# A list scheduler told that four transposes land late, a new shuffle seed, and an unevenly split last output tile

## The chip, the cores and the metric

One core of one Trainium2 chip runs the whole program. The metric is the device time of one execution in microseconds; the kernel before has a median of 276.47 us over three runs (277.43, 276.40, 276.47). The profiled execution, from whose trace all views here are taken, has a span of 275.7 us from first to last instruction, and a mean granted TensorE clock of 0.999.

## The reference

The input x has 2048 tokens of width 640. It is layer-normalised once, and two branches read the normalised xn; their sum is added to x.

```python
x  = A_x
xn = _layernorm(x, axis=-1)
return x + _A_ref(xn, A_wqkv, A_w_phi, A_wo) + _B_ref(xn, B_w1, B_w3, B_w2)

# A: linear attention, 32 heads of 20: q, k, v from xn @ wqkv
phi_q = concat(softmax(q @ w_phi), softmax(-(q @ w_phi)))     # the same for k
kv, z = phi_k^T v, sum over tokens of phi_k
o     = phi_q kv / (phi_q z + 1e-6);  return o @ wo

# B: gated MLP, 640 -> 1536 -> 640
h = silu(xn @ w1) * (xn @ w3);        return h @ w2
```

## The kernel before

**Tiling.** Tokens are cut into 16 tiles of 128, and into 4 blocks of 512. Work for the matrix engine (TensorE, PE in the profile) comes in units, each of which owns one, two or four of the eight PSUM banks. Those that matter here are:

- V and K of a token tile: five chunks of the model width times two halves of 320 columns, 10 matmuls each. They read xnT (the normalised tokens, transposed) and the weights wv and Wkp (wk with w_phi folded in). ScalarE and VectorE drain them to v2 and ekt.
- MLP units "M block.chunk", made by `mlp` (line 1046): 5 matmuls of 512 columns with w1 and 5 with w3, all on one block's xnT. ScalarE makes a tanh, VectorE two products, and the result goes to hT. Units M0.0 to M0.11 belong to block 0, which holds token tiles 0 to 3 only. Unit M0.f reads columns 128f to 128f+127 of w1 and w3.
- kv_sum, kv_back, q_proj and q_tok: the attention itself.
- output tiles O0 to O15, made by `out_tile` (line 1064): 12 chunks of hT times w2 and 5 chunks of oT times wo, times two column groups, 34 matmuls. VectorE adds the residual, and SyncE (SP) stores the tile.

**Start.** Tiles 0 to 3 are transposed on PE. Tiles 4 to 15 are normalised in place in x_tok by `ln_apply`, and then turned by a transposing DMA (`turn`, lines 692, 1165 and 1166) from x_tok into xnT. All these DMAs are on SP's queue, beside the loads of later x tiles, of w1 and w3 (`load_w13`, in pieces of 384 columns, that is three M units each) and the transposing loads of wq and wk (wqkT).

**What sets the order.** The order of each engine's instructions is not written out by hand. `_Program.schedule` (line 171) is a list scheduler with a cost model: it takes every operation's modelled duration, keeps a modelled end for each, and at each step commits the piece of work that can start first. Among those that can start within a small slack, the one with the higher level goes. Levels are due times: `when(us)` is 1000 - us, so V of tile t has due time 20 + 5(t - 4), K the same plus 2, and M0.f 24 + 5f (lines 1178, 1179 and 1193). The slack is drawn at random from a seeded generator up to a modelled time of 175 us; that is what SEED (line 496) decides. For a DMA, the model adds a fixed 1.3 us plus the operation's own `extra` to the modelled end of its transfer:

```python
692    def turn(o, i, level=0.0, dram=False, after=()):
...
695        d.extra = 1.0 if dram else 0.2
```

`extra` is a number inside the model only. Nothing on the chip waits because of it; it moves the point at which the model lets a unit that reads the turned tile be committed. `emit` then writes one fixed list of instructions for each engine, with semaphore waits for the true dependences, and each engine plays its list in order. The 12 DMA-turned tiles have `extra` 0.2.

**The end.** The last output tile, O15, is computed as two separate units of bank work: the first 320 columns with all 17 chunks, then the other 320, each followed by its own addition on VectorE and its own store, so that the first store runs under the second half's matmuls.

Of the kernel before, what the change touches and what calls it, by code (L numbers as in the profile page):

```python
# [5 lines left out]
ALU = mybir.AluOpType  # L6
# [4 lines left out]
D = 640  # L11
# [3 lines left out]
T = S // 128  # L15
# [477 lines left out]
CENTRED = {0: "ACT", 1: "ACT", 2: "ACT", 3: "DVE"}  # L493
POOLED = ()
TURNED = ()
SEED = 65
TRIPLES = ((0, 3, 0, 60), (3, 3, 60, 60), (6, 3, 120, 60), (9, 3, 180, 60), (12, 3, 240, 60), (13, 3, 300, 20))


def bass_parallel_sum__linear_kernel_hedgehog__glu_gated_swiglu__prompt_kernel(  # L500
# [13 lines left out]
    P = _Program(nc)  # L514
# [12 lines left out]
    def new(name, shape, dtype, offset=None):  # L527
        size = mybir.dt.size(dtype)
        for n in shape[1:]:
            size *= n  # L530
        return P.sbuf(name, shape, dtype, region(size) if offset is None else offset)
# [23 lines left out]
    xres = new("xres", [128, 4, D], bf)  # L555
# [42 lines left out]
    def bank(k, cols=512, off=0, p0=0, p1=128):  # L598
        return PS[p0:p1, k * 512 + off:k * 512 + off + cols]

    def bank2(k, cols):
        return PS[:, k * 512:(k + 2) * 512].rearrange("p (b c) -> p b c", c=512)[:, :, 0:cols]

    def free(ap):
        n = 1
        for s in ap.shape[1:]:
            n *= s
        return n
# [6 lines left out]
    def mm(j, o, l, r, start, stop, shared=False, busy=None):  # L615
        u, n = P.unit, free(r)

        def emit():
            return nc.tensor.matmul(o(u.k), l, r, start=start, stop=stop, skip_group_check=shared)  # L619
        return P.mm(emit, [l, r], j, max(n / 2400 + 0.0025, 0.035) if busy is None else busy, n)  # L620

    def way(eng, name, args, kw, busy, lat):
        u = P.unit
        e = {"ACT": nc.scalar, "DVE": nc.vector, "POOL": nc.gpsimd}[eng]

        def emit():
            return getattr(e, name)(*[at(a, u) for a in args], **{k: at(v, u) for k, v in kw.items()})  # L627
        emit.__name__ = name
        return eng, (emit, busy, lat)
# [5 lines left out]
    def sb(*aps):  # L635
        return [a for a in aps if hasattr(a, "ap")]

    def add(ways, w, r, banks=None, level=0.0, after=(), part=False):
        o = P.op(dict(ways), sb(*w), sb(*r), banks, level, after)
        o.part = part  # L640
        return o
# [11 lines left out]
    def w_tt(eng, o, a, b, f, n, fast=1):  # L653
        if eng == "DVE":
            return way(eng, "tensor_tensor", (o, a, b, f), {}, 0.07 + n / 960 / fast, 0.15 + n / 960 / fast)
        return way(eng, "tensor_tensor", (o, a, b, f), {}, 0.14 + n * 1.7 / 1000, 0.18 + n * 1.7 / 1000)
# [25 lines left out]
    def pieces(o, elem):  # L682
        n = 1
        for s in o.shape:
            n *= s
        return n * 2 / elem / 16, max(18.5, 12 + 0.04 * elem) / 1e3

    def load(o, i, level=0.0, eng="SP", after=()):
        return P.dma(eng, lambda: queue[eng].dma_start(o, i), sb(o), sb(i), *pieces(o, 2 * o.shape[-1]), 0.45, level,  # L689
                     after)  # L690

    def turn(o, i, level=0.0, dram=False, after=()):
        d = P.dma("SP", lambda: nc.sync.dma_start_transpose(o, i), sb(o), sb(i), *pieces(o, 256),
                  1.31, level, after)
        d.extra = 1.0 if dram else 0.2
        return d
# [4 lines left out]
    out_t = out.rearrange("b (t p) d -> p (b t) d", p=128)  # L701
# [18 lines left out]
    def load_wT(which, e, level, after=()):  # L720
        return turn(wqkT[:, which * DC + e:which * DC + e + 1, :],
                    A_wqkv[:, which * D + 128 * e:which * D + 128 * e + 128], level, True, after)
# [42 lines left out]
    def ln_stats(t0, n, level):  # L765
        for t in range(t0, t0 + n):
            for q in range(2):
                i, o = x_tok[:, t, 320 * q:320 * q + 320], bst[:, t, 6 * q:6 * q + 6]
                add([w_op("DVE", "bn_stats", (o, i), 0.48, 0.5)], [o], [i], None, level)
            o, i = mv[:, t, 0:2], bst[:, t, 0:12]  # L770
            add([w_op("DVE", "bn_aggr", (o, i), 0.13, 0.21)], [o], [i], None, level)
        m, v, r, z = mv[:, t0:t0 + n, 0], mv[:, t0:t0 + n, 1], mv[:, t0:t0 + n, 4], mv[:, t0:t0 + n, 6]
        add([w_op("POOL", "tensor_scalar_add", (r, v, EPS), 0.21, 0.25)], [r], [v], None, level)
        add([w_op("POOL", "tensor_tensor", (r, r, mhalf[:, 0:n], ALU.pow), 0.55 + 0.1 * (n - 1),
                  0.6 + 0.1 * (n - 1))], [r], [r, mhalf[:, 0:n]], None, level)
        if t0 >= 4:
            add([w_op("POOL", "tensor_scalar_mul", (z, m, -1.0), 0.21, 0.25)], [z], [m], None, level)
            add([w_op("POOL", "tensor_tensor", (z, z, r, ALU.mult), 0.21, 0.25)], [z], [z, r], None, level)

    def ln_apply(t, level):  # L780
        o, m, s, z = x_tok[:, t, :], mv[:, t, 0:1], mv[:, t, 4:5], mv[:, t, 6:7]
        ways = [w_op("DVE", "tensor_scalar", (o, o, m, s, ALU.subtract, ALU.mult), 0.35, 0.44)]
        if t in POOLED:
            ways = [w_op("POOL", "tensor_scalar", (o, o, m, s, ALU.subtract, ALU.mult), 2.5, 2.55)]
        if t >= 4:
            ways.append(w_act(o, o, ACT.Identity, D, s, z))
        add(ways, [o], [o, m, s, z] if t >= 4 else [o, m, s], None, level)
# [274 lines left out]
    finish = []  # L1062

    def out_tile(t, level):
        b, ti = divmod(t, 4)
        u = P.begin(2, level, stream="O")
        u.name = f"O{t}"
        chunks = [(hT[b][:, i, ti * 128:(ti + 1) * 128], w2_s, i) for i in range(FC)]
        chunks += [(oT[:, i, t * 128:(t + 1) * 128], wo_s, i) for i in range(DC)]
        r = xres[:, t % 4, :].rearrange("p (b c) -> p b c", c=320)  # L1070
        load(xres[:, t % 4, :], x_t[:, t, :], 2e5 - 2 * t)
        if t < 4:
            P.all[-1].early = 60.0
        last = t == T - 1
        for qs in ([(0,), (1,)] if last else [(0, 1)]):
            for n, (l, w, i) in enumerate(chunks):
                for q in qs:
                    mm(q, lambda k, q=q: bank(k + q, 320), l, w[:, i, 320 * q:320 * q + 320], n == 0,
                       n == len(chunks) - 1)
            if last:  # L1080
                q = qs[0]
                add([w_tt("DVE", r[:, q, :], lambda k, q=q: bank(k + q, 320), r[:, q, :], ALU.add, 320)],
                    [r[:, q, :]], [r[:, q, :]], [q], 2e6)
                finish.append(load(out_t[:, t, 320 * q:320 * q + 320], r[:, q, :], 3e5))
            else:
                if qs[0] == 0:
                    add([w_tt("DVE", r, lambda k: bank2(k, 320), r, ALU.add, D)], [xres[:, t % 4, :]],
                        [xres[:, t % 4, :]], [0, 1], 1e6)
                    finish.append(load(out_t[:, t, :], xres[:, t % 4, :], 3e5 - 2 * t))

    def filler(t, until):
        u = P.begin(1, 0.0)
# [36 lines left out]
    for e in range(DC):  # L1129
        o = load_wT(1, e, lv - 9 - e, first)  # L1130
    load_x(4, 8, lv - 19, "SP", [o])
    n = len(P.all)
# [14 lines left out]
    n = len(P.all)  # L1147
# [13 lines left out]
    for t in range(4, T, 2):  # L1161
        ln_stats(t, 2, 1e5 - t)
        ln_apply(t, 2e5 - t)
        ln_apply(t + 1, 2e5 - t)
        turn(xnT[:, :, t * 128:(t + 1) * 128], x_tok[:, t, :], lv)
        turn(xnT[:, :, t * 128 + 128:(t + 2) * 128], x_tok[:, t + 1, :], lv)

    def when(us):
        return 1000.0 - us
# [11 lines left out]
    n = len(P.all)  # L1181
# [8 lines left out]
    for b in range(3):  # L1190
        for fc in range(FC):
            n = 12 * b + fc
# [6 lines left out]
    for b in range(NB):  # L1199
        for j in range(4):  # L1200
            t = 4 * b + j
# [4 lines left out]
    for t in range(T):  # L1206
        out_tile(t, when(200 + 5 * t))

    P.schedule({"PE": 1.25, "ACT": 1.12, "DVE": 0.93, "POOL": 0.8, "SP": 0.81}, filler, 12.0, SEED, 175.0)

# [60 lines left out]
```

The softmax here doesn't subtract the row's maximum and nothing guards it: scores larger than these inputs give would overflow.

## Time and profile before

| what | value |
|---|---|
| median time, range of three | 276.47 us, 276.40 to 277.43 us |
| span of the profiled execution | 275.7 us |
| VectorE, ScalarE, GpSimd busy | 183.7, 102.8, 60.4 us |
| DMA traffic | 21.98 MB, mean 80 GB/s |
| V of tile 4 starts on PE | 39.06 us |
| last matmul's result ready | about 273.05 us |

The span is split into 40 slices of 6.9 us in the page's busy rows, where a digit is tenths of the slice. "Idle before, releaser" is the time that an engine stood still ahead of an instruction, and what ended that wait by the trace's semaphore events; where several semaphores were waited for, the one named is the one that came last near that moment, and it can be a bystander. "To landing" of a DMA counts from its issue to the moment when its semaphore is complete.

### The profile page before, as it was taken

How to read it: one execution, taken by the hardware profiler on the slowest of the kernel's cores; microseconds unless marked ns; L12 is line 12 of the kernel's file. 1: busy time of each engine (PE TensorE's matmuls, PEld its weight loads, DVE VectorE, ACT ScalarE, POOL GpSimd, SP SyncE). 2: the span in 40 equal slices, each digit the busy share in tenths (PEclk: the TensorE clock that was granted, in tenths of full speed). 3: DMA queues.
4: the chain of work that ended last, by engine and by line, in shares of the span. 5: the costliest groups of instructions: out<-in, count | busy, mean ns of one | idle time of the engine just before them, and what ended most of it. 6: DMA issues, size and time to landing. Idle time of an engine off the chain costs nothing.

```text
span 275.7 us, 5062 instructions
## 1 busy us (share of the span) xinstructions
PE 267.7 (97%) x2085; PEld 159.5 (58%) x2104; DVE 183.7 (67%) x322; ACT 102.8 (37%) x188; POOL 60.4 (22%) x101
## 2 busy tenths in 40 slices
PE   8999979999999999999999999999999999999996
PEld 4747437765664446644444445777677774444774
DVE  5848886999999544478759986277677215666212
ACT  6637618874445441237393364010110002322000
POOL 4500632699989800000000000000000000000000
PEclk9999999999999999999999999999999999999999
DMA  7568998672000000702131111234443322000001
GB/s 233 153 95 275 343 165 174 106 205 74 0 0 2 0 0 2 259 30 26 24 50 22 26 26 26 71 95 75 108 111 84 85 71 74 0 0 0 26 24 48
DMA packets 41287, 21.98 MB, mean 80 GB/s; under 512 B 27056, under 2 KB 41264, under 8 KB 41264
## 3 DMA queue, kind: packets, MB, share of 16 engines
q1 hardware_dynamic: 40688, 21.01, 31.4%
q10 hardware_dynamic: 576, 0.66, 0.7%
q8 instruction: 16, 0.26, 0.4%
q14 instruction: 7, 0.06, 0.1%
HBM read 12.81 MB, written 2.62 MB: 56 GB/s over the span
## 4 chain that ended last, share of the span: by engine, by line
PE 90%; DVE 4%; DMA 2%; issue 1%; ACT 1%; ACTq 0%; DVEq 0%
PE PS L619 89%; DMA x_tok<-in_A_x_dram 2%; DVE hT L627 1%; DVE t L627 1%; DVE prod L627 1%; DVE bst L627 0%; PE PS L857 0%; DVE den_s L627 0%; ACTq L689 0%; DVE Wqp L627 0%; ACT th L627 0%; ACT EqT L627 0%; ACT L627 0%; DVE xres L627 0%; ACT e_s L627 0%
## 5 line engine op out<-in xcount | busy, mean ns | idle before, releaser
L619 PE MATMUL PS<-xnT,w_s 128*128 128x512 bf16 x464 | 104.9, 379 | 1.2 <-issue 0.5
L619 PEld LDWEIGHTS PS<-xnT,w_s 128*128 128x128 bf16 x480 | 46.4, 98 | 54.1 <-DVE hT L627 0.3
L619 PE MATMUL PS<-w_s,hT 128*128 128x320 bf16 x384 | 55.0, 299 | 0.0
L627 ACT ACTIVATE th<-PS 128x512 f32<-128x512 f32 x48 | 28.7, 599 | 63.9 <-PE PS L619 63.7
L627 DVE SCALAR_TENSOR_TENSOR t<-th,PS 128x512 bf16<-128x512 f32 x48 | 32.9, 684 | 26.2 <-ACT th L627 26.0
L619 PEld LDWEIGHTS PS<-w_s,hT 128*128 128x128 bf16 x384 | 37.0, 98 | 14.9
L627 POOL TENSOR_TENSOR ekt<-ekt,rS 128x640 bf16<-128x640 bf16 x32 | 39.6, 1272 | 1.9 <-DVE rS L627 1.9
L627 DVE TENSOR_TENSOR xres<-PS,xres 128x640 bf16<-128x640 f32 (+1 forms) x17 | 13.4, 786 | 39.0 <-PE PS L619 39.0
L627 DVE SCALAR_TENSOR_TENSOR hT<-t,PS 128x512 bf16<-128x512 bf16 x48 | 32.6, 679 | 1.3 <-DVE t L627 0.2
L627 ACT ACTIVATE EqT<-PS 128x512 bf16<-128x512 f32 x40 | 21.9, 595 | 12.0 <-PE PS L619 12.0
L627 ACT ACTIVATE e_s<-PS 128x64 f32<-128x64 f32 x32 | 9.1, 284 | 44.3 <-PE PS L619 43.9
L619 PE MATMUL PS<-wo_s,oT 128*128 128x320 bf16 x160 | 24.5, 299 | 0.0
L627 DVE TENSOR_TENSOR prod<-PS,g_s 128x1280 bf16<-128x1280 f32 x16 | 23.9, 1491 | 0.5
L619 PE MATMUL PS<-Wkp,xnT 128*128 128x320 bf16 x160 | 23.9, 299 | 0.0
L627 ACT ACTIVATE ekt<-PS 128x640 bf16<-128x640 f32 x32 | 20.8, 702 | 7.7 <-PE PS L619 7.5
L619 PE MATMUL PS<-xnT,Wqp 128*128 128x512 bf16 x97 | 22.9, 379 | 0.3 <-issue 0.2
L627 DVE TENSOR_REDUCE S<-ekt 128x64 f32<-128x1280 bf16 x16 | 22.8, 1450 | 0.0
L619 PE MATMUL PS<-wv,xnT 128*128 128x320 bf16 x120 | 18.3, 299 | 1.9 <-DVE mv L627 1.9
L619 PEld LDWEIGHTS PS<-wo_s,oT 128*128 128x128 bf16 x160 | 15.7, 98 | 6.1
L619 PEld LDWEIGHTS PS<-Wkp,xnT 128*128 128x128 bf16 x160 | 15.5, 98 | 6.1 <-ACT Wkp L627 0.2
L627 DVE BATCH_NORM_STATS2 bst<-x_tok 128x6 f32<-128x320 bf16 x32 | 14.2, 472 | 3.9 <-DMA x_tok<-in_A_x_dram 3.8
L619 PEld LDWEIGHTS PS<-wv,xnT 128*128 128x128 bf16 x120 | 11.7, 98 | 7.5 <-DVE mv L627 2.4
(69 smaller groups left out, 167.2 us busy)
## 6 DMA issues: line engine op xcount, KB each, us to landing
w_s<-in_B_w_dram SPq DMA_DIRECT2D x8, 480.0 KB, 7.5
xres<-in_A_x_dram SPq DMA_DIRECT2D x16, 160.0 KB, 2.2
out_dram<-xres SPq DMA_DIRECT2D x15, 160.0 KB, 1.8
x_tok<-in_A_x_dram SPq DMA_DIRECT2D x3, 640.0 KB, 7.6
w_s<-in_B_w_dram SPq DMA_DIRECT2D x1, 1920.0 KB, 8.9
wo_s<-in_A_wo_dram SPq DMA_DIRECT2D x1, 800.0 KB, 5.1
x_tok<-in_A_x_dram SPq DMA_DIRECT2D x2, 160.0 KB, 3.6
x_tok<-in_A_x_dram ACTq DMA_DIRECT2D x2, 160.0 KB, 4.4
```

Of the source, the lines that this page charges most:

```text
L619: return nc.tensor.matmul(o(u.k), l, r, start=start, stop=stop, skip_group_check=shared)
L627: return getattr(e, name)(*[at(a, u) for a in args], **{k: at(v, u) for k, v in kw.items()})
```

## The change

Three edits. First, the transposes of token tiles 4 to 7 (the loop runs over tile pairs 4-5, 6-7 and so on) get `extra` = 8.0 in place of 0.2, so that the scheduler believes that they land 7.8 us later than before. V and K of tile 4 then look unready for longer, and the scheduler fills the time with MLP units of block 0, whose tiles are there: units M0.3 to M0.9 go ahead of V and K of tile 4, where M0.3 to M0.6 did before. It is meant to bring the model's landing nearer to the chip's. Second, the seed of the shuffled slack is another one, which may reorder any close decision before 175 us of modelled time. Third, the last output tile is cut 384 and 256 columns, not 320 and 320, so that what follows the last matmul is a smaller addition and a smaller store. The rest of the diff in `out_tile` is the same code in another shape: tiles 0 to 14 are as before.

```diff
-SEED = 65
+SEED = 1008
...
-        last = t == T - 1
-        for qs in ([(0,), (1,)] if last else [(0, 1)]):
+        if t < T - 1:
             for n, (l, w, i) in enumerate(chunks):
-                for q in qs:
+                for q in range(2):
                     mm(q, lambda k, q=q: bank(k + q, 320), l, w[:, i, 320 * q:320 * q + 320], n == 0,
                        n == len(chunks) - 1)
-            if last:
-                q = qs[0]
-                add([w_tt("DVE", r[:, q, :], lambda k, q=q: bank(k + q, 320), r[:, q, :], ALU.add, 320)],
-                    [r[:, q, :]], [r[:, q, :]], [q], 2e6)
-                finish.append(load(out_t[:, t, 320 * q:320 * q + 320], r[:, q, :], 3e5))
...
+            return
+        for q, c0, c1 in ((0, 0, 384), (1, 384, D)):
+            for n, (l, w, i) in enumerate(chunks):
+                mm(q, lambda k, q=q, c=c1 - c0: bank(k + q, c), l, w[:, i, c0:c1], n == 0, n == len(chunks) - 1)
+            o = xres[:, t % 4, c0:c1]
+            add([w_tt("DVE", o, lambda k, q=q, c=c1 - c0: bank(k + q, c), o, ALU.add, c1 - c0)], [o], [o], [q], 2e6)
+            finish.append(load(out_t[:, t, c0:c1], o, 3e5))
...
         turn(xnT[:, :, t * 128:(t + 1) * 128], x_tok[:, t, :], lv)
         turn(xnT[:, :, t * 128 + 128:(t + 2) * 128], x_tok[:, t + 1, :], lv)
+        if t < 8:
+            for d in P.all[-2:]:
+                d.extra = 8.0
```

More of the change, by code (lines that the diff above doesn't have):

```diff
@@ L1073, in out_tile @@
             P.all[-1].early = 60.0
-        last = t == T - 1
-        for qs in ([(0,), (1,)] if last else [(0, 1)]):
+        if t < T - 1:
             for n, (l, w, i) in enumerate(chunks):
-                for q in qs:
+                for q in range(2):
                     mm(q, lambda k, q=q: bank(k + q, 320), l, w[:, i, 320 * q:320 * q + 320], n == 0,
                        n == len(chunks) - 1)
-            if last:
-                q = qs[0]
-                add([w_tt("DVE", r[:, q, :], lambda k, q=q: bank(k + q, 320), r[:, q, :], ALU.add, 320)],
-                    [r[:, q, :]], [r[:, q, :]], [q], 2e6)
-                finish.append(load(out_t[:, t, 320 * q:320 * q + 320], r[:, q, :], 3e5))
[L1085 to L1089, printed above, removed]
+            add([w_tt("DVE", r, lambda k: bank2(k, 320), r, ALU.add, D)], [xres[:, t % 4, :]],
+                [xres[:, t % 4, :]], [0, 1], 1e6)
+            finish.append(load(out_t[:, t, :], xres[:, t % 4, :], 3e5 - 2 * t))
+            return
[5 more added lines that the diff above has]
+            finish.append(load(out_t[:, t, c0:c1], o, 3e5))
     def filler(t, until):
```

## Prediction

> **What bounds the kernel now.** I read the page's shares first, then PE's waits, then PE's timeline around the longest wait, then the landings of the DMAs that this wait hangs on, and last the end of the timeline.
>
> ```profile
> PE 267.7 (97%) x2085; PEld 159.5 (58%) x2104; DVE 183.7 (67%) x322; ACT 102.8 (37%) x188; POOL 60.4 (22%) x101
> PEclk9999999999999999999999999999999999999999
> PE 90%; DVE 4%; DMA 2%; issue 1%; ACT 1%; ACTq 0%; DVEq 0%
> ```
>
> PE is busy for 97% of the span at full clock and is 90% of the chain that ended last: only PE's idle time and its number of columns can be saved. The change leaves the columns alone, so everything lies in 275.7 - 267.7 = 8.0 us of idle time. By stretches it is:
>
> ```profile
> 14.70:28.50 13.80, 13.73 (x99) 1.00 0.79 202
> 28.50:37.10 8.60, 8.56 (x39) 1.00 1.14 273
> 37.10:39.06 1.96, 0.02 (x1) 1.00 1.35 144
> 39.06:107.00 67.94, 67.42 (x420) 1.00 0.30 65
> 107.00:175.00 68.00, 67.10 (x670) 1.00 0.22 52
> 175.00:273.03 98.03, 97.86 (x757) 1.00 0.22 59
> 273.03:275.70 2.67, 0.00 (x0) 0.89 0.11 31
> ```
>
> (Columns: stretch, its length, PE busy with instructions, clock, DMA share, GB/s.) One hole of 1.94 us stands out, the tail is 2.67, and from 39 to 175 us some 1.4 us lie in crumbs. The hole on PE's timeline:
>
> ```profile
> 28.54 8.58 PE L619 MATMUL PS<-xnT,w_s 128*128 128x512 bf16 x39
> 39.06 1.52 PE L619 MATMUL PS<-wv,xnT 128*128 128x320 bf16 x10 [1.94 <-DVE mv L627]
> 40.42 1.52 PE L619 MATMUL PS<-Wkp,xnT 128*128 128x320 bf16 x10
> ```
>
> These are M0.3 to M0.6 (40 matmuls, 39 recorded), then V and K of tile 4, V of tile 5 and so on. V of tile 4 reads xnT of tile 4. The releaser named, a VectorE statistic, only fell at that moment: V doesn't read it. The transpose of that tile, asked for alone, reads
>
> ```profile
> L693 SPq DMA_TRANSPOSE xnT<-x_tok x1: 3127/3127/3127, 28.9 to 28.9; - x1
> DMA to landing us min/median/max: 10.0/10.0/10.0
> ```
>
> so it was issued at 28.95 and landed near 38.95, 0.1 us before V starts. A transpose issued at 44.4 lands in 2.7 us: this one was late because the queue ahead of it was full. The last x load (25.46, 10.4 us to landing) and a w1 load (27.12, 10.1 us) were still moving, and the DMA share was above 1.
>
> **What the Trainium skill says.** "DMA: Bandwidth & Descriptors", section on queues, rings and completion order: on each DMA engine descriptors are consumed in ring order. The 10.0 against 2.7 us agrees. "TensorE: Matmul & The Clock Gate", section on what happens when you issue a matmul: matmuls stay in program order, only weight loads are pulled ahead; so one unready V stops the M units listed behind it. The hole agrees. The same page, section on the back-to-back gap: N/2.4 + 2.5 ns; for 512 columns 216 ns, and the trace has 8.58 us for 40, 215 ns; for 320 columns 136 ns, and the trace has 10 per 1.36 us.
>
> **The change, part by part.**
>
> 1. *M0.7 to M0.9 go ahead of V4.* This adds no work: three units of 10 x 0.215 = 2.15 us, 6.45 us in all, come forward from after 61 us. M0.3 to M0.9 run from 28.54 to 28.54 + 7 x 2.15 = 43.6. The transposes of tiles 4 to 7 were issued at 28.95, 32.07, 35.7 and 37.1 and took 10.0, 7.8, 4.9 and 4.1 us: landed at 38.95, 39.9, 40.6 and 41.2. All precede 43.6, so V4 waits for nothing: -1.94 us.
>
> 2. *What the units need.* w1 and w3 columns 768 to 1151 (M0.6 to M0.8) landed at 22.5 + 8.5 = 31.0 and 23.9 + 10.2 = 34.1; M0.7 starts at 37.1, free. M0.9 needs columns 1152 on: w1 landed at 27.12 + 10.1 = 37.2. The w3 piece was issued only after the four transposes, at 38.55, and landed 4.1 us later, at 42.65. M0.9 starts at 28.54 + 6 x 2.15 = 41.4, its w3 half at 42.5: a new wait of some 0.15 us if SP keeps its order. Queued behind it are the second half of M0.9 and then V4; all of PE would wait. Bounds 0 (w3 goes earlier) and, if all four wqkT transposes issued after it (39.18 to 44.33) went first, 5.15 us more. I take +0.15, since both have the same inputs and levels as before.
>
> 3. *VectorE and ScalarE.* Three units bring 3 x (0.684 + 0.679) = 4.1 us of VectorE forward. From 37.1 to 43.6 VectorE was busy 3.9 of 6.5 us, so about 1.5 us of statistics and norms are pushed back. Who waits: the later transposes and with them V8. It ran at 49.9 with its transpose landed at 44.4 + 2.7 = 47.1; now it runs some 4.5 us later, at 54.4. Even a delay of all 4.1 us is hidden. In return 60 to 70 us, where VectorE was 9.9 of 10 us busy and PE waited 0.26 us for Wqp, gets lighter: 0 to -0.26, I take -0.1.
>
> 4. *K norms.* GpSimd's norms start up to 4.5 us later; they ended at 95.4 and kv_sum starts at 107.2: hidden.
>
> 5. *Last tile.* 17 x (162.5 + 109.2) ns = 17 x 2 x 135.8 = 4.62 us: no change on PE. The first part ends 17 x 64/2400 = 0.45 us later, its addition and store lie under the 1.86 us of the second: nothing. Behind the last matmul: latency 299 ns at 320 columns, and by the slope to 379 at 512 it is 272 at 256, -0.03. The addition: 0.49 us at 320 and 0.82 at 640, so 0.43 at 256, -0.07. The store moves 64 in place of 80 KB; at the 340 GB/s that the core moved from 30 to 33 us that is -0.05, or nothing if its 1.6 us are all latency; I take -0.02. Its rows become 512 bytes, the least that "DMA: Bandwidth & Descriptors", specifications, gives for full rate; no run here shows smaller ones. Sum -0.12, bounds -0.1 to -0.15.
>
> 6. *The seed.* It redraws near ties up to 175 us. What it can win is bounded by the crumbs: 0.5 + 0.9 us from 39 to 175, and 0.1 from 14.7 to 37. What it can lose the profile does not bound: any unready unit in an in-order queue is a new hole, and the 1.94 us is the one size that I have for one. I take 0, with about 0.8 us either way.
>
> Sum: -1.94 + 0.15 - 0.1 - 0.12 = -2.0. From 276.47, **274.5 us**, 0.7% faster.
>
> **The rivals.**
>
> *The hole is partly given back.* Order is redrawn everywhere, and crumbs of 0.16 us (there are four such waits "for issue") or a wait of half the old size return, about 1.2 us. For it: the model that misjudged tile 4 still judges all else. Against: from 39 to 273 us PE always had a ready unit in its list, 1.6 us idle in 234, and M units of other blocks remain as fill. It gives 275.7, no difference that can be told.
>
> *The wait moves to the w3 piece of M0.9.* If SP puts it behind two of the wqkT transposes, it lands 2 x 1.28 = 2.6 us later, and PE waits 2.7 us where it waited 1.94. For it: SP was held 9.6 us by four transposes, so it runs late and the piece has only -0.15 us of slack. Against: the piece went before them. With the gain at the tail and a little lost to the seed this gives 277.3, slower; with all four ahead, 276.5 + 5.15 - 1.8 = 279.8.
>
> *The start shortens too.* Up to 14.7 us PE is filled with dummy matmuls between the first tiles, and another draw can bring M0.0 forward by some tenths: 273.6. Against: the third tile's data land at 8.43, whatever the order.
>
> **How the numbers follow.** Forecast (274.5) 0.60, start or crumbs better too (273.6) 0.08, given back (275.7) 0.19, wait moved (277.3 and over) 0.13. The first two are faster by over 0.5% (below 275.1), but the forecast's seed term of 0.8 us reaches over that bound in a small part: faster 0.66. No change is 275.1 to 277.9: the third, and that part, and the milder half of the fourth: same 0.24. The rest, slower, 0.10. The range holds the first three cases and the mild end of the fourth: 273.3 to 276.9.
>
> **What would show it.** Step 1: from 28.5 us seven M units in a row to near 43.6, then V of tile 4 with no idle time ahead; PE's waits without an entry near 2 us. Step 2: M0.9's sixth matmul within 0.3 us of its fifth; a longer hole near 42.5 would be the wait moved. Steps 3 and 4: no idle ahead of V8 to V15 and of kv_sum. Step 5: the addition of the last tile near 0.43 us, and 2.5 to 2.6 us from the last matmul to the end. Step 6: PE idle from 39 to 175 us within 0.8 us of the old 1.4. I am wrong if the start of M0.0 moves by over half a microsecond, or if a hole of over 1 us stands anywhere between 14 and 273 us.

## The result, and the profile after

The changed kernel takes 274.76 us (median of 4, 274.39 to 275.16) beside 276.60 us for the kernel before: ratio 0.9928, 95% interval 0.9901 to 0.9955. A second measurement (e5 below) gave 0.9926 (0.9904 to 0.9949). The forecast was 274.5 us, with a range of 273.3 to 276.9.

The page of the kernel after, engines and chain:

```profile
PE 268.7 (99%) x2103; PEld 159.5 (59%) x2103; DVE 183.9 (67%) x323; ACT 102.1 (37%) x187; POOL 61.2 (22%) x101
PE 96%; DMA 2%; DVE 1%; ACTq 0%; issue 0%; ACT 0%
```

PE has gone from 97% to 99% of the span and from 90% to 96% of the chain. Not all of the first step is real. The kernel before has records of 2085 matmuls for 2104 weight loads, this one 2103 for 2103, and a missing record counts as idle time; the profiled run of e5, the same kernel with 2085 matmuls recorded, shows 98%. PE's waits of the kernel after are one line, the wait for the zeros of the dummy matmuls at 1.3 us:

```profile
PE PS L1098 <- DVE zero L627: 1.3, 1, 1.3
```

PE's timeline after, from the first MLP unit to K of tile 4 (start, length, instruction, count):

```profile
14.10 6.64 PE L619 MATMUL PS<-xnT,w_s 128*128 128x512 bf16 x30
...
27.93 15.27 PE L619 MATMUL PS<-xnT,w_s 128*128 128x512 bf16 x70
43.03 1.52 PE L619 MATMUL PS<-wv,xnT 128*128 128x320 bf16 x10
44.39 1.52 PE L619 MATMUL PS<-Wkp,xnT 128*128 128x320 bf16 x10
```

Seven units (70 matmuls) stand where four stood, and V of tile 4 follows with no idle time. Busy time by stretches after (stretch, length, PE busy with count, clock, DMA share, GB/s):

```profile
37.10:39.06 1.96, 1.96 (x11) 1.00 1.15 306
39.06:43.60 4.54, 4.54 (x25) 1.00 0.87 154
43.60:107.00 63.40, 63.40 (x425) 1.00 0.23 50
107.00:175.00 68.00, 67.98 (x689) 1.00 0.24 55
```

The hole is filled. The crumbs between 107 and 175 us are gone too, but they were missing records, not idle time. In the kernel before, all four "issue" waits of 0.16 us stand ahead of groups that show 9, 19 or 29 matmuls of units that have 10, 20 or 30. Two of them:

```profile
112.25 2.11 PE L619 MATMUL PS<-xnT,w_s 128*128 128x512 bf16 x9 [0.16 <-issue]
153.81 6.42 PE L619 MATMUL PS<-xnT,w_s 128*128 128x512 bf16 x29 [0.16 <-issue]
```

Hardly any of those 0.9 us was there to be won.

SP's timeline after around the transposes, and the landings of tile 4's transpose and of the last w3 piece, each asked for alone:

```profile
29.00 5.79 SPq L693 DMA_TRANSPOSE xnT<-x_tok  x2
34.84 0.58 SPq L689 DMA_DIRECT2D w_s<-in_B_w_dram  x1
35.46 2.69 SPq L693 DMA_TRANSPOSE xnT<-x_tok  x2
```

```profile
DMA to landing us min/median/max: 8.1/8.1/8.1
```

```profile
DMA to landing us min/median/max: 4.4/4.4/4.4
```

Tile 4 landed at 29.0 + 8.1 = 37.1 us, and the w3 piece, now ahead of the transposes of tiles 6 and 7, at 34.84 + 4.4 = 39.2 us, before its use at about 42.

**Where the time went.** Between fixed marks of the two profiled executions, with the spans to two digits from the traces; three units are 30 x 0.2157 = 6.47 us:

| from, to | before | after | difference |
|---|---|---|---|
| start to V of tile 3 | 13.14 | 12.73 | -0.41 |
| V of tile 3 to V of tile 4, less the three units moved | 25.92 | 30.30 - 6.47 | -2.09 |
| V of tile 4 to the last addition, plus the three units | 234.00 | 227.18 + 6.47 | -0.35 |
| last addition to the end | 2.60 | 2.47 | -0.13 |
| span | 275.65 | 272.68 | -2.97 |

The spans differ by 3.0 us and the medians by only 1.8. The profiled run of before was a late one (277.37 us) and that of after the earliest (274.39). The first row points to a reason: the x tile on ScalarE's queue landed 6.08 us after its issue in one and 5.22 in the other. Other runs of the two kernels have no trace, so where their landings lay isn't known. The profiled run of e5, the same kernel with a landing of 5.89 us, has a span of 273.3.

### The profile page after: what moved, and what is told of

Its sections match the earlier page's. It is cut to its first block, busy times and chain, and to the rows that moved or that the text cites. A ratio compares the mean times of both kernels' runs of the same rounds, so it can differ in the third digit from the quotient of the medians.

```text
span 272.7 us, 5086 instructions
## 1 busy us (share of the span) xinstructions
PE 268.7 (99%) x2103; PEld 159.5 (59%) x2103; DVE 183.9 (67%) x323; ACT 102.1 (37%) x187; POOL 61.2 (22%) x101
## 4 chain that ended last, share of the span: by engine, by line
PE 96%; DMA 2%; DVE 1%; ACTq 0%; issue 0%; ACT 0%
PE PS L619 95%; DMA x_tok<-in_A_x_dram 2%; PE PS L857 1%; ACTq L689 0%; ACT L627 0%; PE PS L1098 0%; DVE xres L627 0%; DVE bst L627 0%; DVE xc L627 0%; DVE x_tok L627 0%; PE PS L810 0%; DVE mv L627 0%
## 5 line engine op out<-in xcount | busy, mean ns | idle before, releaser
L619 PE MATMUL PS<-xnT,w_s 128*128 128x512 bf16 x480 | 106.8, 379 | 0.0
L619 PE MATMUL PS<-w_s,hT 128*128 128x320 bf16 (+2 forms) x384 | 55.0, 299 | 0.0
L627 DVE TENSOR_TENSOR xres<-PS,xres 128x640 bf16<-128x640 f32 (+2 forms) x17 | 13.4, 786 | 39.9 <-PE PS L619 39.9
L619 PE MATMUL PS<-wo_s,oT 128*128 128x320 bf16 (+2 forms) x160 | 24.5, 299 | 0.0
L619 PE MATMUL PS<-xnT,Wqp 128*128 128x512 bf16 x100 | 23.6, 380 | 0.0
L619 PEld LDWEIGHTS PS<-xnT,Wqp 128*128 128x128 bf16 x100 | 9.3, 98 | 10.8
```

## Experiments

Ratios are to the kernel before on the same chip, with the 95% interval. "Units" are the M units listed between K of tile 3 and V of tile 4, "hole" is PE's idle time ahead of V of tile 4 in the profiled run. The ratios of e5 to e8 share one set of eleven runs of the kernel before, and one of those took 278.93 us where the others took 276.84 to 277.38; without it these four ratios would be about 0.0006 higher. No reading below hangs on that.

| run | seed, extra, last tile | units | hole, us | median, us | ratio |
|---|---|---|---|---|---|
| before | 65, 0.2, 320+320 | 4 | 1.94 | 276.6 to 277.0 | 1 |
| changed, e5 | 1008, 8, 384+256 | 7 | 0 | 275.16 | 0.9926 (0.9904 to 0.9949) |
| e1 | 65, 8, 320+320 | 7 | 0 | 275.30 | 0.9941 (0.9929 to 0.9953) |
| e2 | 1008, 0.2, 320+320 | 3 | 3.13 | 280.28 | 1.0119 (1.0087 to 1.0151) |
| e3 | 1008, 8, 320+320 | 7 | 0 | 275.33 | 0.9947 (0.9934 to 0.9961) |
| e4 | 1008, 4, 384+256 | 5 | 0 | 275.50 | 0.9953 (0.9942 to 0.9965) |
| e6 | 65, 6, 384+256 | 6 | 0 | 274.89 | 0.9913 (0.9892 to 0.9935) |
| e7 | 65, 0.2, 320+320, loads held back | 4 | 0 | 274.92 | 0.9917 (0.9894 to 0.9940) |
| e8 | 65, 6, 512+128 | 6 | 0 | 275.09 | 0.9919 (0.9898 to 0.9940) |
| e9 | 65, -1, 320+320 | 3 | 3.34 | 281.25 | 1.0178 (1.0162 to 1.0195) |
| e10 | as e2 | 3 | 3.40 | 280.22 | 1.0111 (1.0084 to 1.0139) |
| e11 | 1008, 12, 384+256 | 9 | 0 | 275.57 | 0.9953 (0.9940 to 0.9967) |

**e1, the late landing alone.**

```diff
 (the kernel before)
+        if t < 8:
+            for d in P.all[-2:]:
+                d.extra = 8.0
```

> The kernel before with the late landing alone (extra 8.0 for tiles 4 to 7); seed 65 and the even last tile stay. Its list puts seven M units ahead of V4, and SP keeps the order of before, with the last w3 piece behind all four transposes. Theory (the hole is the gain): no idle time ahead of V4, which starts 6.45 us later than the old place less the 1.94 us hole; a wait of 0.1 to 0.4 us inside M0.9 for the w3 piece; time 0.6 to 0.7% under the kernel before, ratio 0.993 to 0.995. Rival (the new seed's order is the gain): ratio 0.998 to 1.002. Rival (the gain was a lucky start of the profiled run and noise): ratio 0.998 to 1.002.

Measured: 275.30 us, ratio 0.9941. The late landing alone carries most of the gain, with the old seed and the old last tile. PE's timeline of e1 shows the new wait that the prediction was after (the last column is idle time before, and its releaser):

```profile
28.42 13.98 PE L619 MATMUL PS<-xnT,w_s 128*128 128x512 bf16 x63
42.77 1.24 PE L619 MATMUL PS<-xnT,w_s 128*128 128x512 bf16 x5 [0.38 <-DMA w_s<-in_B_w_dram]
43.85 1.52 PE L619 MATMUL PS<-wv,xnT 128*128 128x320 bf16 x10
```

The second half of M0.9 waits 0.38 us for its w3 piece, which SP issued at 38.30, behind the four transposes, and which landed 4.3 us later. In the changed kernel this wait isn't there, because the piece was issued between the transposes. e2 has that issue order too, with the new seed and the old extra.

**e2, the seed alone.**

```diff
-SEED = 65
+SEED = 1008
```

> The kernel before with seed 1008 alone. Its list puts only three M units ahead of V4, one fewer than before, and the last w3 piece between the transposes of tiles 5 and 6. Theory (the hole is the gain): three units end near 28 + 6.45 = 34.5 us and the transpose of tile 4 lands between 37 and 39, so the hole ahead of V4 grows to 2.5 to 4.3 us and the kernel is 0.6 to 2.3 us slower than before: ratio 1.002 to 1.008. Rival (the seed is the gain): ratio 0.992 to 0.995.

Measured: 280.28 us (278.58 to 282.04), slower. The rival that the seed brings the gain is out. By itself this seed lists only three units ahead of V of tile 4, and the hole grows:

```profile
38.55 1.52 PE L619 MATMUL PS<-wv,xnT 128*128 128x320 bf16 x10 [3.13 <-DVE mv L627]
```

The profiled run (278.95 us, span 277.2) is slower than that of before by 1.6 us: the hole is 1.2 longer, and the start accounts for nearly all the rest, 0.45 us (see e5). But four of the six runs took 280.1 to 282.0 us, more than the expectation allowed. e9 and e10 went after that.

**e3, the last tile even again.**

```diff
-        for q, c0, c1 in ((0, 0, 384), (1, 384, D)):
+        for q, c0, c1 in ((0, 0, 320), (1, 320, D)):
```

> The changed kernel with the last output tile cut 320 and 320 again. Theory: everything to the last tile as in the changed kernel; from the last matmul to the end 0.1 to 0.15 us longer than with 384 and 256 (addition 0.49 in place of 0.42 us); ratio to the kernel before 0.9925 to 0.994. Rival (the uneven cut carries a good part of the gain): ratio 0.996 or more.

Measured: 275.33 us, ratio 0.9947, a little over the range expected. From the start of its last addition (271.02) to the end it takes 2.60 us, where the changed kernel has 2.47 and 2.46 in its two profiled runs. The uneven cut is worth 0.13 to 0.14 us, which times alone can't tell from nothing.

**e4, five units in place of seven.**

```diff
-                d.extra = 8.0
+                d.extra = 4.0
```

> The changed kernel with extra 4.0 in place of 8.0: five M units (M0.3 to M0.7) go ahead of V4. Theory: they end near 27.9 + 10.75 = 38.7 us, after tile 4 has landed (37.1 us in the changed kernel), so no hole or one below 0.3 us, and the time of the changed kernel: ratio to before 0.992 to 0.995. Rival (all seven units have to go ahead): a hole of over 1 us ahead of V4 or V5 and ratio 0.996 or more.

Measured: 275.50 us, ratio 0.9953. V of tile 4 starts at 39.09 without a wait:

```profile
28.51 10.74 PE L619 MATMUL PS<-xnT,w_s 128*128 128x512 bf16 x49
39.09 1.52 PE L619 MATMUL PS<-wv,xnT 128*128 128x320 bf16 x10
```

Five units are enough to close the hole in this run. The transpose landed at 30.0 + 8.3 = 38.3 us, 0.8 us before its use. The ratio lies just over the expected range; two waits of 0.2 to 0.3 us for VectorE's products stand among PE's waits here and not in the changed kernel.

**e5, the changed kernel again.** No edit.

> The changed kernel as it is, to stand beside the others on one chip, and for a second look at its start. Theory: the profiled run of the changed kernel began early because the x tile loaded last landed 5.2 us after issue where others took 5.6 to 6.1; with a usual landing M0.0 starts near 15.1 us (14.7 in the kernel before), and the ratio to before is 0.992 to 0.996. Rival (the new seed makes the start earlier): M0.0 at 14.1 us again.

Measured: 275.16 us, ratio 0.9926. M0.0 starts at 14.8 us (V of tile 3 at 13.41, plus its 1.36), not at 14.1 again. The start was set by a landing, and the new seed's order costs time there, it doesn't save any. V of tile 3, less the landing of the x tile on ScalarE's queue, in the profiled runs:

| seed | run: V of tile 3 - landing, us |
|---|---|
| 65 | before 13.14 - 6.08 = 7.06; e1 13.02 - 5.95 = 7.07; e7 13.33 - 6.26 = 7.07; e8 13.40 - 6.33 = 7.07; e9 13.40 - 6.34 = 7.06 |
| 1008 | after 12.73 - 5.22 = 7.51; e2 13.59 - 6.08 = 7.51; e3 13.55 - 6.03 = 7.52; e4 13.10 - 5.58 = 7.52; e5 13.41 - 5.89 = 7.52; e10 12.95 - 5.45 = 7.50; e11 13.91 - 6.38 = 7.53 |

Only e6 is left out: its chain up to M0.0 waits for no load. Seed 1008 starts 0.45 us later at the same landing. VectorE's timeline of e5 shows what it drew differently: it gives VectorE the copy of tile 0's transpose, ahead of the centring of tile 3, and the kernel before left that copy to ScalarE:

```profile
10.59 0.48 DVE L627 COPY xnT<-PS 128x640 bf16<-128x640 bf16 x1
10.98 0.20 DVE L627 BATCH_NORM_AGGREGATE mv<-bst 128x2 f32<-128x12 f32 x1
11.22 0.39 DVE L627 TENSOR_SCALAR xc<-x_tok,mv 128x640 bf16<-128x640 bf16 x1
```

On ScalarE, in the kernel before:

```profile
10.54 0.70 ACT L627 ACTIVATE xnT<-PS 128x640 bf16<-128x640 bf16 x1
```

The centring of tile 3 starts 2.50 us after the landing in the kernel before and 2.97 in e5. The copy (0.48 us) accounts for that difference; no run moves the copy alone. So the early start of the first profiled run was the landing: 0.86 us earlier, less 0.45 for the order, is the -0.41 of the table above.

**e6, six units and the old seed.**

```diff
-SEED = 1008
+SEED = 65
...
-                d.extra = 8.0
+                d.extra = 6.0
```

> The changed kernel with seed 65 and extra 6.0: six M units (M0.3 to M0.8) ahead of V4, none of which needs the last w3 piece, and the start of the kernel before. Theory: no hole ahead of V4 (six units end near 41.4 us, tile 4 lands near 39), no wait in M0.9, the start of seed 65 (M0.0 at 14.6 to 14.8 us): 0.3 to 0.6 us faster than the changed kernel with a usual landing, ratio to before 0.990 to 0.994. Rival (seed 1008 has the better order elsewhere): slower than the changed kernel.

Measured: 274.89 us, ratio 0.9913, the lowest of all, but the interval holds that of e5 nearly whole: 0.27 us between the medians is not shown. V of tile 4 starts without a wait, at 41.34 us, and M0.9 is not in the row. PE's own work set the start of this run, not a landing, so it isn't in the table of e5.

**e7, the queue cleared instead.** The scheduler's belief stays as before; the loads themselves are held back.

```diff
 (the kernel before)
+    m = len(P.all)
     load_x(12, 16, lv - 23)
     load_w13(1152, 1536, lv - 24)
+    late(m, 31.0)
```

> The kernel before (seed 65, extra 0.2, even tail, four M units ahead of V4 as before), but the load of x tiles 12 to 15 and the last w1 and w3 pieces are held back, so that they are issued after the transposes of tiles 4 to 7: 1.6 MB less stand ahead of those. Theory (the transposes land late because the queue ahead is full): the transpose of tile 4 takes 4 to 6 us in place of 10 and lands before 37.1 us, the hole ahead of V4 is gone without any unit moved, and the kernel is about 1.9 us faster than before: ratio 0.992 to 0.995. Rival (a transposing DMA is slow or V4 waits for something else, a VectorE statistic as the profile names it): the hole stays within 0.5 us of 1.9.

Measured: 274.92 us, ratio 0.9917. SP's timeline, then the landing of tile 4's transpose, then PE's timeline, all of e7:

```profile
25.45 5.23 SPq L693 DMA_TRANSPOSE wqkT<-in_A_wqkv_dram  x2
30.73 6.25 SPq L693 DMA_TRANSPOSE xnT<-x_tok  x4
37.02 0.58 SPq L689 DMA_DIRECT2D x_tok<-in_A_x_dram  x1
```

```profile
DMA to landing us min/median/max: 6.0/6.0/6.0
```

```profile
28.73 8.58 PE L619 MATMUL PS<-xnT,w_s 128*128 128x512 bf16 x39
37.14 1.52 PE L619 MATMUL PS<-wv,xnT 128*128 128x320 bf16 x10
```

This is the run that shows the cause. The transpose of tile 4 was issued 1.8 us later than before (two wqkT transposes slipped ahead of it) and yet landed 2.2 us earlier, at 36.7: 6.0 us in place of 10.0. With four units ahead of V, as before, the hole is gone. The transposes were late because of the loads ahead of them in the queue, and the hole was that lateness; that the M units go ahead is only one of two cures, and the times don't tell the two apart (274.92 and 275.16 us).

**e8, a smaller last piece.**

```diff
 (e6)
-        for q, c0, c1 in ((0, 0, 384), (1, 384, D)):
+        for q, c0, c1 in ((0, 0, 512), (1, 512, D)):
```

> The kernel of e6 with the last output tile cut 512 and 128. Theory: the last addition falls from 0.42 to about 0.29 us, its matmul latency by 0.05, and the store of 32 KB lands in 1.4 to 1.5 us: from the start of the last addition to the end 2.3 to 2.4 us, where 384 and 256 takes 2.5; the time 0.1 to 0.2 us under e6, not to be told from it by times. Rival (rows of 256 bytes, the larger first store or its addition hold the last one up): 2.5 us or more.

Measured: 275.09 us, ratio 0.9919; by the times the same as e6. VectorE's last two additions of e8 (span 273.4):

```profile
270.19 0.69 DVE L627 TENSOR_TENSOR xres<-PS,xres 128x512 bf16<-128x512 f32 x1 [2.84 <-PE PS L619]
271.14 0.29 DVE L627 TENSOR_TENSOR xres<-PS,xres 128x128 bf16<-128x128 f32 x1 [0.26 <-PE PS L619]
```

From 271.14 to the end it takes 2.25 us, against 2.47 in e6: another 0.2 us won at the tail, which a later start of this run (V of tile 3 at 13.40, against 13.21) took back. The last store, 32 KB in rows of 256 bytes, landed in 1.5 us, as did the 64 KB in rows of 512 bytes, so the shorter rows cost nothing that shows here.

**e9, one unit fewer with the old seed.**

```diff
 (the kernel before)
+        if t < 8:
+            for d in P.all[-2:]:
+                d.extra = -1.0
```

> The kernel before (seed 65, even tail) with extra -1.0 for tiles 4 to 7: three M units ahead of V4, one fewer than before. Theory (each unit moved is worth its 2.15 us until the hole is gone): the hole is 1.9 + 2.15 = 4.1 us, and the kernel 2.1 to 2.5 us slower than before, ratio 1.0075 to 1.009. A second theory, for e2 being 3.4 us slower where its profiled run explains 1.6: a hole as long as this also lets the granted TensorE clock fall for some microseconds, which would show below 1.0 in the slices after the hole and add 0.5 to 2 us: ratio 1.009 to 1.016. Rival (e2 was slow from its seed): ratio below 1.0075.

Measured: 281.25 us (279.44 to 282.19), ratio 1.0178: slower than either theory allowed. The profiled run is the fastest of the five, 2.1 us above that of before, with the clock at 1.00. Its hole is 3.34 us and not 4.1: the transpose landed 0.4 us earlier than in the profiled run of before, and the three units ended 0.3 us later than the sum behind 4.1 has them. Of the 2.1 us, 1.4 are the longer hole, 0.3 a later start, and 0.4 net lie behind V of tile 4, where a wait of 0.5 us for hT has come up. The hole is put down here to the DMA itself:

```profile
38.56 1.53 PE L619 MATMUL PS<-wv,xnT 128*128 128x320 bf16 x10 [3.34 <-DMA xnT<-x_tok]
```

The old seed is slow too when one unit is taken away, so the long hole of e2 needs no fault of its seed beyond the missing unit. What the slower runs lost, e10 shows.

**e10, e2 once more.** No further edit.

> The kernel of e2 once more, for another profiled run. If the landing of tile 4's transpose varies, hole and time vary together: a run above 280 us should show a hole of over 4 us, or a clock below 1.0 after it. If neither is there, its excess over 1.6 us comes from elsewhere. Ratio as in e2, 1.008 to 1.016.

Measured: 280.22 us. This time the profiled run (280.20 us) is one of the slower kind. PE's timeline of e10, and its stretches:

```profile
38.18 2.30 PE L619 MATMUL PS<-wv,xnT 128*128 128x320 bf16 x10 [3.40 <-DMA xnT<-x_tok]
40.28 2.46 PE L619 MATMUL PS<-Wkp,xnT 128*128 128x320 bf16 x10
42.57 1.52 PE L619 MATMUL PS<-wv,xnT 128*128 128x320 bf16 x10
```

```profile
38.00:39.00 1.00, 0.82 (x6) 0.88 1.10 310
39.00:42.00 3.00, 3.00 (x13) 0.50 1.18 227
42.00:43.00 1.00, 1.00 (x9) 0.92 0.90 189
```

After a hole of 3.40 us the granted clock falls to 0.50 for some 3.4 us. V and K of tile 4 take 42.57 - 38.18 = 4.39 us where 2 x 1.36 = 2.72 is their time, and 1.67 us are lost on top of the hole. In e2 and e9, at 3.13 and 3.34 us, the clock did not fall in the profiled runs.

The mean clock of every run tells about the others. One fall of 1.67 us takes 0.006 off the mean of a run of 278.5 us, and the profiled run of e10 has 0.994. All the runs with three units ahead of V of tile 4 (e2 and e10 are the same kernel):

| mean clock | e2, us | e9, us | e10, us |
|---|---|---|---|
| 0.999 to 1.000 | 278.58, 278.95 | 279.44 | 278.37 |
| 0.993 to 0.994 | 280.14, 280.41, 280.57 | 281.15, 281.25 | 280.20, 280.25, 280.50 |
| 0.987 to 0.988 | 282.04 | 282.12, 282.19 | |

So ten of the fifteen runs lost clock time, one such fall's worth or about two, and that is what made e2 and e9 slower than their holes explain. The runs of e2 with the full clock are 1.006 to 1.008 of the kernel before, as its theory said. Where in the other runs the clock fell, only a trace would show. One of the 31 runs of the kernel before whose clock is on record has it too: 278.93 us at 0.994. In the 47 runs of the kernels with no such hole (the changed one, e1, e3 to e8, e11) the mean clock is never below 0.999.

The Trainium skill ("TensorE: Matmul & The Clock Gate", the part on the clock gate) says that an idle window of about 3.4 us brings the clock to half, and that the window is free-running. The half agrees (0.50). How long a hole must be isn't settled here: 3.40 us was followed by a fall, 3.34 us was not, and the kernel before, whose hole was 1.94 us when profiled, has no trace of its run of 278.93 us. That the window runs freely no run here shows.

**e11, nine units.**

```diff
-                d.extra = 8.0
+                d.extra = 12.0
```

> The changed kernel with extra 12.0: all nine M units left in block 0 (M0.3 to M0.11) go ahead of V4. Theory: tile 4 has long landed, the weights of M0.9 to M0.11 have too (last w3 piece about 39.5, needed at 42.5), so nothing is gained over eight: PE without a wait to V4 near 47.5 us, time of the changed kernel, ratio 0.991 to 0.996. Rival (too many units ahead starve VectorE or the later K norms, so that kv_sum waits): a new wait after 60 us and ratio 0.997 or more.

Measured: 275.57 us, ratio 0.9953. V of tile 4 starts at 48.53 without a wait, and no wait of over 0.4 us stands on PE anywhere after the start. The profiled run had a late x tile (6.38 us) and a further wait of 0.4 us for wv at 7.98 us, and with them a start 0.5 us later than that of e5. Past the landing, more units neither gain nor visibly cost, though a hidden cost of a few tenths is not ruled out.

## Why the prediction was right or wrong, point by point

**The hole.** Forecast -1.94 us, found -2.09 between V of tile 3 and V of tile 4, and the same in e5. The mechanism was right in every link: a full queue ahead of the transpose (e7), V of tile 4 held by its landing and not by the VectorE statistic that the profile names (e7: the hole went when the landing came forward; e9 and e10 name the DMA), and units put ahead to cover it (e1 and e4: closed; e2 and e9: one unit fewer and it grows). The size was short by 0.15: an idle time is counted from the modelled end of the last matmul, 379 ns after its start, while the next could have started after 216, so each hole costs 0.16 us more than it reads. A small slip beside it: the prediction divides 8.58 us by 40 matmuls, while that row holds 39; the row of 70 runs from 27.93 to 43.03, 215.7 ns each.

**The w3 piece in M0.9.** Forecast +0.15, found 0. The premise that failed is "both have the same inputs and levels as before": SP's order changed, and the piece went between the transposes. That was the luck of the draw. Where the order is the old one, the wait is there, 0.38 us (e1), so the rival that the wait moves to M0.9 was real in kind, and small.

**VectorE.** Forecast -0.1, bounds 0 to -0.26, found about -0.35 from V of tile 4 to the last addition (the same in e5), outside the bounds. The wait that it named is this one of the kernel before, and it is gone:

```profile
66.40 0.80 PE L619 MATMUL PS<-BDc,wqkT 128*128 128x140 bf16 x12 [0.26 <-DVE Wqp L627]
```

By the same rule as the hole it cost 0.26 + 0.16 = 0.42 us; the bound was taken from the reading. Nothing was lost at V of tile 8 or kv_sum, as forecast.

**The last tile.** Forecast -0.12, found -0.13: the addition took 0.42 us, 0.43 forecast, and the store 1.5 us in place of 1.6.

**The seed.** Forecast 0 with 0.8 us either way. At the same landing it costs 0.45 us at the start, and it placed the w3 piece so that the wait of e1 (0.38 us read, 0.54 by the rule above) doesn't arise. The two nearly cancel, so that the forecast of 0 came out near by luck: e1 and e3, which differ in the seed alone, have 275.30 and 275.33 us. What the prediction took for winnable, 0.9 us of crumbs from 107 to 175 us, was missing records.

**The sum.** From the row of differences, with e5's landing in place of the early one: -2.09 - 0.35 - 0.13 + 0.45 = -2.1 at equal landings, against -2.0 forecast and medians 1.8 us apart in both measurements. The total is nearer than its terms: the hole and VectorE were each too small, the w3 piece too dear, and the seed's cost stood at nothing. The prediction named a move of M0.0 by over half a microsecond as a sign that it was wrong. The rows read 14.72 and 14.10, but that of before shows 29 of 30 matmuls and lacks the first: V of tile 3 starts at 13.14 and takes 1.36, so M0.0 started at 14.50. The move was 0.40 us, within the sign, and it is the 0.86 us of an earlier landing outside the change, less the 0.45 of the seed (e5).

## What to carry to other kernels

When a matrix engine that plays a fixed list is nearly full, look for the one hole, and ask for the landing of the transfer behind it rather than for the releaser that is named: here the cure is either to tell the planner the true landing or to clear the queue ahead of the transfer, and both close the hole. Ready work cost nothing visible here when it moved further ahead than needed (e11), so leave a margin of a unit or two. One unit of 2.16 us too few lengthened the hole by 1.2 to 1.5 us (e2, e9, e10), and in ten of fifteen runs the fall of the clock added 1.7 us or more. Before crediting a change with a difference between two profiled runs, subtract what a landing at the start did. And before counting short idle times as a gain to be won, compare the number of matmuls recorded with the number in the program.

## What the runs showed of the hardware

The landing of one 160 KB load at the start varied from 5.2 to 6.4 us over the profiled runs with the same issue order in the first 3 us, and moved the start of V of tile 3 one for one in all of them but e6. The transpose of tile 4, issued into a full queue in all profiled runs but e7, took 8.1 to 10.0 us to land and held SP for 2.5 to 3.1 us, against 2.7 and 1.3 us for transposes issued later on a clear one. An idle stretch of PE of 3.40 us was followed by some 3.4 us at half the clock (0.50), at a cost of 1.67 us; one of 3.34 us, in another run, was not. A matmul of 512 columns takes 379 ns from start to end but the next starts after 216, so an idle time ahead of a matmul reads 0.16 us short of what was lost.
